# A Fourier-mixing and SoLU block on one core: shared even and odd up products, block transposes, and down products by Strassen's scheme

## The chip, the cores and the metric

The kernel runs on one core of a Trainium2 chip, in one launch, in float32 throughout. The metric is the device time of one execution in microseconds (us), median of several. Before the change it is 2172.12 us (three runs, 2170.49 to 2173.72). A profile is one further execution recorded by the hardware; its span is 2166.9 us.

A core has five engines with an instruction queue each: TensorE (PE, matrix products into PSUM), VectorE (DVE), ScalarE (ACT), GpSimd (POOL) and SyncE (SP, which here only issues transfers). They meet through semaphores. PSUM has eight banks of 512 float32 per partition.

## The reference, cut to what matters

```python
x: (8, 3136, 256)                                  # batch, sequence, features
X = np.fft.fft(np.fft.fft(x, axis=1), axis=2).real # 25088 tokens of 256 features
h = X @ w_in                                       # 256 -> 1024
e = np.exp(h - h.max(-1)); sm = e / (e.sum(-1) + 1e-9)
solu = h * sm
ln = (solu - mean(solu)) / np.sqrt(var(solu) + 1e-6) * g_ln
out = ln @ w_out                                   # 1024 -> 256
```

## The kernel before

The sequence transform (length 3136 = 49 x 64) is done in two passes of matrix products, for four pairs of batches. The feature transform is folded into `w_in`. A pair has 25 values of k1; each gives 64 frequencies for both batches, that is 128 tokens, and for k1 > 0 also the 128 tokens of the negative frequencies. In this text a *unit* is one (pair, k1) and a *block* is 128 tokens of one sign: 100 units, 196 blocks, 96 units of two blocks.

The first pass (`fold`, `transform1`) of the next pair runs in small steps beside the units of the current one, and goes through DRAM (`zd`) to turn its layout. The second pass gives `q`, the unit's 256 folded features on partitions:

```python
    def transform2(pr, k1):
        ps = ps_m.tile([P, KD, P], FP32, tag="m", name="ps2")
        for h in range(KD):
            nc.tensor.matmul(ps[:, h, :], pr.g[:, k1, ...], T[:, k1, :], ...)     # 2 products of 128 columns
        q = {"+": qpool.tile(...)}
        nc.vector.tensor_copy(out=q["+"], in_=ps)
        if k1:                                   # the sine half changes its sign for the negative frequencies
            ...
                nc.scalar.activation(out=o, in_=i, func=ACT.Copy, scale=sg if h else 1.0)
        return q
```

The second part handles one block at a time; `cur` is the block that enters and `prv` the one before it:

```python
    def up_half(t, half):                        # both halves: 4 products of 512 columns per block
        for h in range(KD):
            nc.tensor.matmul(t.h[:, fs], t.q[:, h, :], Wi[:, h, fs], start=(h == 0), stop=(h == KD - 1))

    def solu(t):
        nc.vector.tensor_reduce(out=nmax, in_=t.h, axis=AX.X, op=ALU.max, negate=True)
        nc.scalar.activation(out=t.u, in_=t.h, func=ACT.Exp, bias=nmax, accum_out=esum)
        nc.vector.scalar_tensor_tensor(out=t.u, in0=t.h, scalar=1.0, in1=t.u, ..., accum_out=usum)
        nc.gpsimd.tensor_scalar(out=nmean, in0=usum, scalar1=-1.0 / FF, ...)
        nc.scalar.activation(out=sq, in_=t.u, func=ACT.Square, bias=nmean, accum_out=ssq)
        ...                                      # four small operations on GpSimd give rs, 1 / deviation

    def transpose(t):                            # 8 transposes on TensorE, copied out by ScalarE and VectorE
        for half in range(2):
            tp = ps_t.tile([P, n, P], FP32, tag="t", name="tp")
            ...
    def down(t):
        ps = ps_m.tile([P, D], FP32, tag="m", name="ps_o")
        for c in range(KF):                      # 8 products of 256 columns per block
            nc.tensor.matmul(ps, t.uT[:, c, :], Wo[:, c, :], start=(c == 0), stop=(c == KF - 1))
        nc.vector.tensor_scalar(out=ot, in0=ps, scalar1=t.rs, scalar2=None, op0=ALU.mult)
        ...                                      # two stores of 64 rows

            if cur: up_half(cur, 0)
            if prv: transpose(prv)
            if cur:
                up_half(cur, 1)
                solu(cur)
                if cur.s == "+":
                    ...                          # transform2 of the next unit
                    ahead(pairs[cur.p + 1], cur.k1)      # fold or one transform1 step of the next pair
            if prv: down(prv)
```

PSUM: two `h` tiles of two banks, two banks for `tp` (`ps_t`), and two banks `ps_m` that `ps1` (the result of `transform1`), `ps2` and `ps_o` take in turn. Before the loop, the weights, which come as the bits of float64 numbers, are narrowed to float32 on VectorE, after the first pair's first pass.

Of the kernel before, what the change touches and what calls it, by code (L numbers as in the profile page):

```python
# [10 lines left out]
I32 = mybir.dt.int32  # L11
ALU = mybir.AluOpType
# [4 lines left out]
P = 128  # L17
# The sequence index is n = N2 * n1 + n2 and its frequency k = k1 + N1 * k2.
# The frequencies k1 of 0..NK-1 are computed; k1 and N1 - k1 share their products.
# [5 lines left out]
CH = 8  # L25
NC = NH // CH

# The layout of the 256 folded features: cosine part at 0..128, sine part (1..127) at 129..255.
# [4 lines left out]
def kernel(  # L33
# [13 lines left out]
    """Sequence DFT with even and odd folds, feature DFT folded into w_in, then SoLU and its layer norm.  # L47

    With U the cosine transform over the sequence of x folded evenly in the features, and V the sine
    transform of x folded oddly, the real part of the 2D DFT is U C - V S at frequency k and U C + V S  # L50
    at -k. So h = [U, V] @ [C w_in; -S w_in], and for -k the features of V change their sign.
    """
# [10 lines left out]
    out_b = out.rearrange("(b s) d -> b s d", b=B)  # L63
# [4 lines left out]
    gpool = ctx.enter_context(tc.tile_pool(name="gpool", bufs=2))  # L68
    qpool = ctx.enter_context(tc.tile_pool(name="qpool", bufs=3))
    small = ctx.enter_context(tc.tile_pool(name="small", bufs=4))  # L70
    dram = ctx.enter_context(tc.tile_pool(name="dram", bufs=2, space=bass.MemoryType.DRAM))
    ps_h = ctx.enter_context(tc.tile_pool(name="ps_h", bufs=2, space=PSUM))
    ps_t = ctx.enter_context(tc.tile_pool(name="ps_t", bufs=2, space=PSUM))
    ps_m = ctx.enter_context(tc.tile_pool(name="ps_m", bufs=2, space=PSUM))

    F = const.tile([PR, 6, ZR], FP32, name="F")
    T = const.tile([P, NK, P], FP32, name="T")
    Wi = const.tile([P, KD, FF], FP32, name="Wi")
    Wo = const.tile([P, KF, D], FP32, name="Wo")
    ident = const.tile([P, P], FP32, name="ident")  # L80
    ones = const.tile([P, P], FP32, name="ones")
    neg_half = const.tile([P, 1], FP32, name="neg_half")
    idx = const.tile([PR, NP * NC], I32, name="idx")
    sg = const.tile([P, 1], FP32, name="sg")

# [1 line left out]

    class Pair:
        def __init__(self, p):
            self.p = p  # L90
            self.raw, self.y, self.y0 = {}, {}, None
            self.g = None

    def load(pr, c):
        """Rows n2 = 8c + 1 .. 8c + 8, and those of S - n beside them (in descending order of n2)."""
        r = slice(pr.p * PR, (pr.p + 1) * PR)
        xa = xpool.tile([PR, CH, D], FP32, tag="xa", name="xa")
        xb = xpool.tile([PR, CH, D], FP32, tag="xb", name="xb")
        nc.sync.dma_start(out=xa, in_=x_pn[r, c * CH + 1 : (c + 1) * CH + 1, :])
        i = pr.p * NC + c  # L100
        nc.gpsimd.indirect_dma_start(
            out=xb.rearrange("p l d -> p (l d)"), out_offset=None, in_=x_g,
            in_offset=bass.IndirectOffsetOnAxis(ap=idx[:, i : i + 1], axis=0))
        x0 = None
        if c == NC - 1:
            x0 = xpool.tile([PR, 1, D], FP32, tag="x0", name="x0", bufs=1)
            nc.sync.dma_start(out=x0, in_=x_pn[r, 0:1, :])
        pr.raw[c] = (xa, xb, x0)

    def fold_features(o, i):  # L110
# [3 lines left out]
        nc.vector.tensor_copy(out=o[:, :, 0:129:128], in_=i[:, :, 0:129:128])  # L114

    def fold(pr, c):
        """x[n, d] + x[-n, -d], then its even and odd parts in d. Rows n2 = 0 and 32 hold their own mirrors."""
        xa, xb, x0 = pr.raw.pop(c)
        n = CH - 1 if c == NC - 1 else CH
        a, rb = xa[:, 0:n, :], xb[:, ::-1, :][:, 0:n, :]  # L120
        nc.gpsimd.tensor_tensor(out=a[:, :, 1:D], in0=a[:, :, 1:D], in1=rb[:, :, D - 1 : 0 : -1], op=ALU.add)  # L121
        nc.gpsimd.tensor_tensor(out=a[:, :, 0:1], in0=a[:, :, 0:1], in1=rb[:, :, 0:1], op=ALU.add)
        y = xpool.tile([PR, CH, D], FP32, tag="y", name="y")
        fold_features(y, xa)
        pr.y[c] = y
        if c == NC - 1:
            pr.y0 = xpool.tile([PR, 1, D], FP32, tag="y0", name="y0", bufs=1)
            fold_features(pr.y0, x0)

    def transform1(pr, s):  # L130
        """Sum over n1 for rows n2 = 2s + 1, 2s + 2; out: (b, cosine or sine, k1) on partitions.

        The last row holds n2 = 0, of no sine part, in its cosine part and n2 = 32 in its sine part."""
# [3 lines left out]
        if l == 0:  # L137
            pr.z = zpool.tile([ZR, CH, D], FP32, tag="z", name="z")
        y = pr.y[c]
        ps = ps_m.tile([P, 2, D], FP32, tag="m", name="ps1")  # L140
        if s == NH // 2 - 1:
            parts = [(ps[0:ZR, 0], y[:, l], 0), (ps[0:ZR, 1], pr.y0[:, 0], 1), (ps[0:ZR, 1], y[:, l + 1], 2)]
        else:
            parts = [(ps[0:ZR], y[:, l : l + 2], 0)]
        first = True
# [6 lines left out]
        if l == CH - 2:  # L152
            nc.sync.dma_start(out=pr.zd[:, c * CH : (c + 1) * CH, :], in_=pr.z)

    def turn(pr):
        """(b, cosine or sine, n2) onto partitions."""
        pr.g = gpool.tile([P, NK, D], FP32, tag="g", name="g")
        for j in range(4):
            nc.sync.dma_start(out=pr.g[j * NH : (j + 1) * NH, :, :],
                              in_=pr.zd[j * NK : (j + 1) * NK, :, :].rearrange("k n d -> n k d"))  # L160

    def transform2(pr, k1):
        """Sum over n2 for both batches; out: folded features on partitions, tokens (b, k2) free."""
        ps = ps_m.tile([P, KD, P], FP32, tag="m", name="ps2")
        for h in range(KD):
            nc.tensor.matmul(ps[:, h, :], pr.g[:, k1, h * P : (h + 1) * P], T[:, k1, :],  # L166
                             start=(h == 0), stop=(h == KD - 1), skip_group_check=True)
        q = {"+": qpool.tile([P, KD, P], FP32, tag="q", name="q")}
        nc.vector.tensor_copy(out=q["+"], in_=ps)  # L169
        if k1:  # L170
            # -(k1 + 49 k2) is (49 - k1) + 49 (63 - k2): the negative frequencies run backwards.
            q["-"] = qpool.tile([P, KD, P], FP32, tag="qm", name="qm")
            for h in range(KD):
                o = q["-"][:, h, :].rearrange("p (b k) -> p b k", b=2)
                i = ps[:, h, :].rearrange("p (b k) -> p b k", b=2)[:, :, ::-1]
                nc.scalar.activation(out=o, in_=i, func=ACT.Copy, scale=sg if h else 1.0)  # L176
        return q

# [1 line left out]

    class Tokens:
        def __init__(self, p, k1, s):
            self.p, self.k1, self.s = p, k1, s

    def up_half(t, half):
        if half == 0:
            t.h = ps_h.tile([P, FF], FP32, tag="h", name="h")
        fs = slice(half * HW, (half + 1) * HW)
        for h in range(KD):
            nc.tensor.matmul(t.h[:, fs], t.q[:, h, :], Wi[:, h, fs], start=(h == 0), stop=(h == KD - 1))  # L190

    def solu(t):
        """u = h exp(h - max h), its sum and centred sum of squares, and the sum of the exponentials."""
        nmax = small.tile([P, 1], FP32, tag="nmax", name="nmax")
        nc.vector.tensor_reduce(out=nmax, in_=t.h, axis=AX.X, op=ALU.max, negate=True)  # L195
        t.u = fpool.tile([P, FF], FP32, tag="u", name="u")
        esum = small.tile([P, 1], FP32, tag="esum", name="esum")
        nc.scalar.activation(out=t.u, in_=t.h, func=ACT.Exp, bias=nmax, accum_out=esum)  # L198
        usum = small.tile([P, 1], FP32, tag="usum", name="usum")
        nc.vector.scalar_tensor_tensor(out=t.u, in0=t.h, scalar=1.0, in1=t.u, op0=ALU.mult, op1=ALU.mult,  # L200
                                       accum_out=usum)
        nmean = small.tile([P, 1], FP32, tag="nmean", name="nmean")
        nc.gpsimd.tensor_scalar(out=nmean, in0=usum, scalar1=-1.0 / FF, scalar2=None, op0=ALU.mult)  # L203
        sq = fpool.tile([P, FF], FP32, tag="sq", name="sq", bufs=1)
        ssq = small.tile([P, 1], FP32, tag="ssq", name="ssq")
        nc.scalar.activation(out=sq, in_=t.u, func=ACT.Square, bias=nmean, accum_out=ssq)  # L206
        # 1 / (sum * sqrt(var(u / sum) + 1e-6)) = (var(u) + 1e-6 sum^2) ** -0.5
        es = small.tile([P, 1], FP32, tag="es", name="es")
        nc.gpsimd.tensor_scalar(out=es, in0=esum, scalar1=1e-9, scalar2=1e-3, op0=ALU.add, op1=ALU.mult)
        es2 = small.tile([P, 1], FP32, tag="es2", name="es2")  # L210
        nc.gpsimd.tensor_tensor(out=es2, in0=es, in1=es, op=ALU.mult)
        v = small.tile([P, 1], FP32, tag="v", name="v")
# [238 lines left out]
```

## Time and profile before

| | |
|---|---|
| time, median of 3 | 2172.12 us |
| span of the profile | 2166.9 us |
| TensorE busy | 1788.7 us |
| VectorE busy | 846.8 us |
| ScalarE busy | 670.6 us |
| GpSimd busy | 382.0 us |
| first `ps_o` product starts | 151.1 us |

How to read what follows. A line such as `L235 PE MATMUL ps_o<-Wo,uT 128*128 128x256 f32 x3136 | 833.5, 425 | 270.8 <- ...` is a group of instructions of line 235: engine, operation, output and inputs by their names in the program, shape, count; then the busy time in us and the mean of one in ns; then the idle time of the engine just before them and what ended it. A float32 product appears as two records: 1568 down products are 3136 records. Records of TensorE overlap (each ends long after the next began), so the time that a stretch takes is read from the distance of starts, not from the durations. PEld is the load of the stationary operand, which runs beside the products. In the row of 40 slices a digit is a busy share in tenths (9 is 90% or more), and PEclk is the clock that TensorE was granted, in tenths of full speed.

### The profile page before, as it was taken

How to read it: one execution, taken by the hardware profiler on the slowest of the kernel's cores; microseconds unless marked ns; L12 is line 12 of the kernel's file. 1: busy time of each engine (PE TensorE's matmuls, PEld its weight loads, DVE VectorE, ACT ScalarE, POOL GpSimd, SP SyncE). 2: the span in 40 equal slices, each digit the busy share in tenths (PEclk: the TensorE clock that was granted, in tenths of full speed). 3: DMA queues.
4: the chain of work that ended last, by engine and by line, in shares of the span. 5: the costliest groups of instructions: out<-in, count | busy, mean ns of one | idle time of the engine just before them, and what ended most of it. 6: DMA issues, size and time to landing. Idle time of an engine off the chain costs nothing. (4 is left out here: it accounts for less than half of the span.)

```text
span 2166.9 us, 19414 instructions
## 1 busy us (share of the span) xinstructions
PE 1788.7 (83%) x6992; PEld 1238.2 (57%) x6992; DVE 846.8 (39%) x1327; ACT 670.6 (31%) x1240; POOL 382.0 (18%) x1034
## 2 busy tenths in 40 slices
PE   2357888788799878878879987887887999999998
PEld 1135555555566555555556755555555666777666
DVE  2853233323334323332433433333233344444444
ACT  1113223223333322332332323233233234434443
POOL 3002121212112212121211221212121111111111
PEclk8679899889899888888999988889899899999999
DMA  9511010001042101000104210101010400000000
GB/s 240 133 33 42 24 46 13 25 13 28 10 90 75 42 20 50 12 26 12 28 11 88 77 42 16 54 10 28 11 29 11 88 18 18 17 16 18 18 18 17
DMA packets 56783, 84.78 MB, mean 39 GB/s; under 512 B 12038, under 2 KB 50574, under 8 KB 51696
## 3 DMA queue, kind: packets, MB, share of 16 engines
q1 hardware_dynamic: 48528, 65.19, 12.7%
q0 software_dynamic: 2048, 12.85, 2.1%
q10 hardware_dynamic: 6112, 5.52, 1.3%
q8 instruction: 55, 0.90, 0.2%
q14 instruction: 40, 0.33, 0.1%
HBM read 44.72 MB, written 38.80 MB: 39 GB/s over the span
## 5 line engine op out<-in xcount | busy, mean ns | idle before, releaser
L235 PE MATMUL ps_o<-Wo,uT 128*128 128x256 f32 x3136 | 833.5, 425 | 270.8 <-ACT qm L176 215.9
L235 PEld LDWEIGHTS ps_o<-Wo,uT 128*128 128x128 f32 x3136 | 668.7, 217 | 444.7 <-ACT qm L176 235.5
L198 ACT ACTIVATE u<-h,nmax 128x1024 f32<-128x1024 f32 x196 | 218.4, 1114 | 634.3 <-DVE nmax L195 634.3
L190 PE MATMUL h<-Wi,q 128*128 128x512 f32 x800 | 384.4, 604 | 7.8 <-DVE q L169 7.8
L190 PE MATMUL h<-Wi,qm 128*128 128x512 f32 x768 | 361.1, 592 | 0.0
L200 DVE SCALAR_TENSOR_TENSOR u<-h,u 128x1024 f32<-128x1024 f32 x196 | 240.0, 1225 | 249.4 <-ACT u L198 249.4
L206 ACT ACTIVATE sq<-u,nmean 128x1024 f32<-128x1024 f32 x196 | 225.1, 1148 | 317.7 <-POOL nmean L203 317.7
L195 DVE TENSOR_REDUCE nmax<-h 128x1 f32<-128x1024 f32 x196 | 239.9, 1224 | 193.5 <-PE h L190 193.5
L203 POOL TENSOR_SCALAR nmean<-usum 128x1 f32<-128x1 f32 x196 | 45.7, 233 | 1515.3 <-DVE u L200 1515.3
L228 DVE COPY uT<-tp 128x512 f32<-128x512 f32 x196 | 135.5, 691 | 372.3 <-PE tp L224 372.3
L230 ACT COPY uT<-tp 128x512 f32<-128x512 f32 x196 | 114.9, 586 | 415.9 <-PE tp L224 415.9
L224 PEld LDWEIGHTS tp<-ident,u 128*128 128x128 f32 x1568 | 183.5, 141 | 104.5 <-issue 103.7
L237 DVE TENSOR_SCALAR ot<-ps_o,rs 128x256 f32<-128x256 f32 x196 | 94.0, 480 | 369.4 <-issue 364.3
L190 PEld LDWEIGHTS h<-Wi,q 128*128 128x128 f32 x800 | 147.5, 195 | 115.4 <-issue 103.7
L224 PE MATMUL tp<-ident,u 128*128 128x128 f32 x1568 | 203.2, 273 | 0.5 <-DVE u L200 0.5
L190 PEld LDWEIGHTS h<-Wi,qm 128*128 128x128 f32 x768 | 138.4, 190 | 96.8 <-issue 91.8
L215 POOL TENSOR_TENSOR rs<-v,neg_half 128x1 f32<-128x1 f32 x196 | 113.2, 578 | 16.3
L148 PE MATMUL ps<-y,F 98*100 98x258 f32 (+3 forms) x288 | 71.5, 385 | 43.3 <-DVE y L114 43.3
L166 PEld LDWEIGHTS ps<-T,g 128*128 128x128 f32 x400 | 60.4, 191 | 47.4 <-issue 47.4
L213 POOL TENSOR_SCALAR v<-ssq,es 128x1 f32<-128x1 f32 x196 | 52.4, 267 | 177.6 <-ACT sq L206 175.5
L148 PEld LDWEIGHTS ps<-y,F 98*100 98x100 f32 x288 | 45.5, 178 | 54.7 <-DVE y L114 30.4
L121 POOL TENSOR_TENSOR xa<-xa,xb 98x2040 f32<-98x2040 f32 (+1 forms) x16 | 70.1, 4379 | 28.9 <-DMA xa<-in_x_dram 16.2
(50 smaller groups left out, 544.4 us busy)
## 6 DMA issues: line engine op xcount, KB each, us to landing
out_dram<-ot SPq DMA_DIRECT2D x392, 64.0 KB
zd<-z SPq DMA_DIRECT2D x16, 800.0 KB
g<-zd SPq DMA_DIRECT2D x16, 800.0 KB
xa<-in_x_dram SPq DMA_DIRECT2D x16, 784.0 KB
raw_in_moe_w_in_dram<-in_moe_w_in_dram ACTq DMA_DIRECT2D x1, 2048.0 KB
raw_in_moe_w_out_dram<-in_moe_w_out_dram ACTq DMA_DIRECT2D x1, 2048.0 KB
T<-in_t_tab_dram ACTq DMA_DIRECT2D x2, 400.0 KB
x<-in_x_dram SPq DMA_DIRECT2D x4, 98.0 KB
```

The source lines that it names most:

```text
L148: nc.tensor.matmul(o[..., cs], F[:, 2 * t + h, :], i[..., cs], start=first, stop=True, skip_group_check=True)
L190: nc.tensor.matmul(t.h[:, fs], t.q[:, h, :], Wi[:, h, fs], start=(h == 0), stop=(h == KD - 1))
L195: nc.vector.tensor_reduce(out=nmax, in_=t.h, axis=AX.X, op=ALU.max, negate=True)
L198: nc.scalar.activation(out=t.u, in_=t.h, func=ACT.Exp, bias=nmax, accum_out=esum)
L200: nc.vector.scalar_tensor_tensor(out=t.u, in0=t.h, scalar=1.0, in1=t.u, op0=ALU.mult, op1=ALU.mult, accum_out=usum)
L206: nc.scalar.activation(out=sq, in_=t.u, func=ACT.Square, bias=nmean, accum_out=ssq)
L215: nc.gpsimd.tensor_tensor(out=t.rs, in0=v, in1=neg_half, op=ALU.pow)
L224: nc.tensor.matmul(tp[:, c, :], t.u[:, f * P : (f + 1) * P], ident, is_transpose=True, start=(c == 0), stop=(c == n - 1), skip_group_check ...
L228: nc.vector.tensor_copy(out=o, in_=tp)
L230: nc.scalar.copy(o, tp)
L235: nc.tensor.matmul(ps, t.uT[:, c, :], Wo[:, c, :], start=(c == 0), stop=(c == KF - 1))
L237: nc.vector.tensor_scalar(out=ot, in0=ps, scalar1=t.rs, scalar2=None, op0=ALU.mult)
```

## The change

The products of both signs are shared. With E the part of h from the cosine features and O the part from the sine features, h is E + O for one sign and E - O for the other, so each part is computed once per unit. One feature (the middle one) moves from the cosine half to a separate per-token term `w_mid * r`. VectorE then builds both h in SBUF and takes their maxima as it does so. The transposes leave TensorE: VectorE transposes blocks of 32 x 32 within SBUF, and 16 transfers per two units carry the blocks to their partitions. The down products of both signs of a unit form one product of a 256 x 1024 matrix (two signs) with a 1024 x 256 matrix; it is cut into 2 x 2 blocks and done by seven block products in place of eight. Sums of blocks of u are formed on GpSimd, sums of weights once, and results on three PSUM banks; the seven products are spread over two steps of the loop, four units behind the one that enters. The diff is cut to its core; in the loop, conditions are left out and calls condensed.

```diff
@@ parameters, pools @@
-CH = 8
+CH = 4
-    ps_h = ctx.enter_context(tc.tile_pool(name="ps_h", bufs=2, space=PSUM))
-    ps_t = ctx.enter_context(tc.tile_pool(name="ps_t", bufs=2, space=PSUM))
-    ps_m = ctx.enter_context(tc.tile_pool(name="ps_m", bufs=2, space=PSUM))
+    ps_h = ctx.enter_context(tc.tile_pool(name="ps_h", bufs=1, space=PSUM))
+    ps_m = ctx.enter_context(tc.tile_pool(name="ps_m", bufs=1, space=PSUM))
... (first pass: smaller pieces; turn in five parts per pair, on GpSimd's queue)
@@ a unit of both signs @@
+    def up(t, c):
+        ps = ps_h.tile([P, FF], FP32, tag=f"h{c}", name=f"ps_h{c}")
+        for half in range(2):
+            nc.tensor.matmul(ps[:, fs], t.q[:, c * P : (c + 1) * P], Wi[:, c, fs], start=True, stop=True)
+    def even(t, ps):
+        nc.vector.scalar_tensor_tensor(out=t.ev, in0=w_mid, scalar=t.r, in1=ps, op0=ALU.mult, op1=ALU.add)
+    def join(t, s):
+        nc.vector.tensor_tensor_reduce(out=t.h[s], in0=t.h[0] if s else t.ev, in1=t.odd, scale=1.0 if s else -0.5,
+                                       scalar=-3.0e38, op0=ALU.add, op1=ALU.max, accum_out=t.nmax[:, s : s + 1])
+    def expo(t, s):
+        nc.scalar.mul(out=t.neg[:, s : s + 1], in_=t.nmax[:, s : s + 1], mul=-1.0)
+        nc.scalar.activation(out=t.u[s], in_=t.h[s], func=ACT.Exp, bias=t.neg[:, s : s + 1], accum_out=...)
+    def product(t, s):
+        nc.vector.scalar_tensor_tensor(out=t.u[s], in0=t.h[s], scalar=1.0, in1=t.u[s], ..., accum_out=...)
+    def square(t, s):
+        nc.scalar.activation(out=t.h[s], in_=t.u[s], func=ACT.Square, bias=t.usum[...], scale=-float(FF), accum_out=...)
+    def stats(t):
+        ... (one Square and, per sign, one Identity on ScalarE; one power on GpSimd)
+    def turn_blocks(t, s):
+        for o in (s,) if len(t.signs) == 2 else (0, 1):
+            nc.vector.transpose(out=t.batch.v[:, t.w, :, o], in_=t.u[s])
+    def move_blocks(batch, units, engines=(nc.sync,)):
+        for i in range(4):
+            for q in range(4):
+                engines[i % len(engines)].dma_start(out=uT[b, i], in_=v[a, q])
@@ down products of both signs @@
+    def sums(t):
+        for o, a, b, op in ((t.S[:, 0], A21, A22, ALU.add), (t.S[:, 1], t.S[:, 0], A11, ALU.subtract),
+                            (A21, A11, A21, ALU.subtract), (t.S[:, 2], A12, t.S[:, 1], ALU.subtract)):
+            nc.gpsimd.tensor_tensor(out=o, in0=a, in1=b, op=op)
+    def product7(o, a, b, start=False):
+        for c in range(KF // 2):
+            nc.tensor.matmul(o, a[:, c], b[:, c], ...)
+        def p1(self):
+            product7(self.C11, self.A11, Wo[:, 0 : KF // 2, 0:P], True)
+            nc.scalar.copy(self.C21, self.C11)
+        def p5(self):
+            product7(self.P53, self.t.S[:, 0], Ws[:, 0], True)
+            nc.scalar.copy(self.E5, self.P53)
+        def p6(self):
+            product7(self.C21, self.t.S[:, 1], Ws[:, 1])
+            nc.scalar.copy(self.X, self.C21)
+        def p2(self):
+            product7(self.C11, self.A12, Wo[:, KF // 2 :, 0:P])
+            self.scale(0, 0, self.C11)
+        def p7_p3(self):
+            product7(self.C21, self.S3, Ws[:, 2])
+            product7(self.P53, self.t.S[:, 2], Wo[:, KF // 2 :, P:])
+        def sum22(self): nc.vector.tensor_tensor(out=self.C22, in0=self.C21, in1=self.E5, op=ALU.add)
+        def sum12(self): nc.vector.tensor_tensor(out=self.C12, in0=self.P53, in1=self.X, op=ALU.add)
+        def p4(self):
+            product7(self.C21, self.A22, Ws[:, 3])
+            ... (three scalings on ScalarE)
+    def store(t):
+        ... (one indirect store on GpSimd's queue and one on SyncE's per unit)
@@ the loop, from unit 5 on (`old` is four units behind `cur`, `half` one more) @@
+            square(prv), stats(prv)
+            sums(nxt)
+            ps = up(cur, 0)
+            half.p4(); half = Down(old, ...); half.p1()
+            other_pairs(i, ahead_pe)             # a transform1 step of the next pair
+            even(cur, ps)
+            half.p5()
+            store(units[i - lag - 1])
+            cur.odd = up(cur, 1); join(cur, 0)
+            half.p6(); expo(cur, 0); half.p2()
+            second_transform(i + 2)
+            join(cur, 1); expo(cur, 1)
+            half.p7_p3(); product(cur, 0); half.sum22(); product(cur, 1); half.sum12()
+            turn_blocks(cur, s) for both signs; after every second unit move_blocks(...)
+            other_pairs(i, ahead)                # loads and folds of the next pair
```

Units 0 to 3 still take TensorE transposes; the units with k1 = 0 and the very last unit still take plain down products. The preparation is rearranged too: the narrowing of the weights (fewer operations each, partly on ScalarE) now stands between the first pair's folds instead of after them, the result of the first pair's first pass is stored and turned in parts, and the tables of the second transform load in two parts.

## The prediction

> **What bounds the kernel now.** I read the page's shares and its row of slices first, then the chain that ended last, a stretch of TensorE's timeline, the groups by form, and the waits.
>
> ```profile
> PE 1788.7 (83%) x6992; PEld 1238.2 (57%) x6992; DVE 846.8 (39%) x1327; ACT 670.6 (31%) x1240; POOL 382.0 (18%) x1034
> ...
> PE   2357888788799878878879987887887999999998
> ...
> PEclk8679899889899888888999988889899899999999
> ```
>
> TensorE is the only engine near full. It is full with a clock of 0.9 to 1.0 in the last quarter (the last pair, with no first pass beside it), and at 8 tenths with a clock of 8 to 9 tenths before.
>
> ```profile
> 1794.27 3.46 PE ps_o L235 x16
> 1802.03 3.45 PE ps_o L235 x16
> 1810.24 3.46 PE ps_o L235 x16
> ```
>
> The chain in the last pair holds nothing but TensorE. Two blocks, one unit, take 1810.24 - 1794.27 = 15.97 us. The timeline says of what:
>
> ```profile
> 1805.32 1.88 PE L190 MATMUL h<-Wi,q 128*128 128x512 f32 x4
> 1807.04 1.04 PE L224 MATMUL tp<-ident,u 128*128 128x128 f32 x8
> 1807.91 1.88 PE L190 MATMUL h<-Wi,q 128*128 128x512 f32 x4
> 1809.63 0.61 PE L166 MATMUL ps<-T,g 128*128 128x128 f32 x4
> 1810.07 3.62 PE L235 MATMUL ps_o<-Wo,uT 128*128 128x256 f32 x16
> 1813.53 1.88 PE L190 MATMUL h<-Wi,qm 128*128 128x512 f32 x4
> ```
>
> From starts: half an up product 1.72 us, eight transposes 0.87, transform2 0.44, a down product 3.46. So a record of 512 columns repeats every 0.43 us, one of 256 every 0.216, one of 128 every 0.11: time goes by columns. A unit is 4 x 1.72 + 2 x 0.87 + 0.44 + 2 x 3.46 = 15.98, as the chain says.
>
> ```profile
> PE ps_o L235 <- ACT qm L176: 215.9, 48, 4.5
> ```
>
> (Total us, times, longest us.) The other loss before the last pair is a PSUM bank: in the 48 steps with `ps1`, the down product takes the bank of `ps2` and waits for its copies, 4.5 us each; with 54 us behind `uT` that makes 270. The whole adds up: 96 x 15.98 + 4 x 8.2 = 1567, first pass in the loop 48 x 0.86 = 41, waits 270, about 141 before the loop (first `ps_o` at 151.1); of 2167 us some 148 remain, which I give to the lower clock.
>
> **What the Trainium skill says.** "TensorE: Matmul & The Clock Gate", LDWEIGHTS: loading 128 columns takes 128 / 1.2 GHz = 107 ns. Here every record has a load, and 128-column records repeat every 0.109 to 0.11 us: agreement, and no room, as load and stream are just equal there. The same page, Part 1: idle gaps of some 3.4 us drop the clock. The stretch 1850 to 1900 us shows a granted clock of 1.00 with TensorE never idle, 1280 to 1330 shows 0.84 with the 4.5 us waits: agreement. "SBUF — State Buffer", Who interferes with whom: a VectorE operation with two SBUF inputs and a GpSimd operation that reads SBUF exclude each other. The loop before never pairs them (its large VectorE operations read PSUM), so no number here shows it. "DMA: Bandwidth & Descriptors", Why small descriptors are slow: the penalty is said to hold for HBM only. The table T arrives here as 3200 packets of 256 B, median 32 ns and mean 43 ns a packet, beside other loads; nothing here moves from SBUF to SBUF.
>
> **The change, part by part.** For a unit of two blocks:
>
> *TensorE.* Up products: 4 instead of 8 of 512 columns, 3.44 us instead of 6.88: -3.44. Transposes leave: -1.74. Down: 28 products of 128 columns, 56 records x 0.11 = 6.2, instead of 6.92: only -0.75, since 7/8 is all that the scheme can give. transform2 stays at 0.44. Sum 3.44 + 6.2 + 0.44 = 10.0, and 10.9 in the 48 units that carry a transform1 step (4 records of 256 columns, 0.86).
>
> *VectorE.* The durations come from the groups by form:
>
> ```profile
> L200 DVE SCALAR_TENSOR_TENSOR u<-h,u 128x1024 f32<-128x1024 f32 x196 | 240.0, 1225 | 249.4 <-ACT u L198 249.4
> L195 DVE TENSOR_REDUCE nmax<-h 128x1 f32<-128x1024 f32 x196 | 239.9, 1224 | 193.5 <-PE h L190 193.5
> L206 ACT ACTIVATE sq<-u,nmean 128x1024 f32<-128x1024 f32 x196 | 225.1, 1148 | 317.7 <-POOL nmean L203 317.7
> L198 ACT ACTIVATE u<-h,nmax 128x1024 f32<-128x1024 f32 x196 | 218.4, 1114 | 634.3 <-DVE nmax L195 634.3
> L121 POOL TENSOR_TENSOR xa<-xa,xb 98x2040 f32<-98x2040 f32 x12 | 54.2, 4514 | 25.7 <-DMA xa<-in_x_dram 13.0 <-DMA xb<-in_x_dram,idx 12.7
> L176 ACT ACTIVATE qm<-ps,sg 128x128 f32<-128x128 f32 x96 | 34.3, 357 | 0.0
> L176 ACT ACTIVATE qm<-ps 128x128 f32<-128x128 f32 x96 | 24.6, 256 | 0.0
> L121 POOL TENSOR_TENSOR xa<-xa,xb 98x1785 f32<-98x1785 f32 x4 | 15.9, 3972 | 3.3 <-DMA xa<-in_x_dram 3.3
> ```
>
> Seven passes of 1024 columns per unit (even, two joins, two products, two block transposes; I estimate the join and the transpose at the rate of the others, no row shows them) at 1.15 us from start to start (an L200 starts at 1221.17, its accumulator read at 1222.32) are 8.05, and two sums of 128 columns 0.28 each (L112 took 283 ns for 127): 8.6. Before it was 2 x (1.23 + 1.22 + 0.69 + 0.48 + 0.08) + 0.42 = 7.8 per unit. Two waits join it: the first product waits for the exponential of the sign joined before, which with its negation takes about 0.5 us longer than the second join; the second waits behind a scaling, the copy of q, a negation and an exponential, 2.2 us against 1.4 of VectorE work. Chain: 8.6 + 0.5 + 0.8 = 9.9. Folds add 1.4 in 24 of the steps.
>
> *ScalarE.* Exponentials 2 x (1.11 + 0.19), squares 2 x (1.15 + 0.19) = 5.3; three copies at 0.26, four scalings at 0.36, q at 0.37, five tiny operations at 0.15 to 0.25: 3.6. Sum 8.9; with the copy of transform1 (0.59) 9.5.
>
> *GpSimd.* Its slope is (4514 - 3972) / 255 = 2.13 ns per column, its fixed part 0.18 us: four sums of 512 columns 4 x 1.27 = 5.1. Power 0.6, indirect store 1.4, first pass of the next pair (mirror sums, gathers, turning) about 2.2 on average. Sum 9.3, from under 4 before.
>
> So TensorE leads with 10.0 to 10.9, VectorE's chain has 9.9 to 11.3, and two more engines 9: the work is spread evenly, and the bound is a loop through four engines. I **choose** 10.4 us for the 24 units of the last pair, 11.3 with transform1, 10.6 else: (24 x 10.4 + 48 x 11.3 + 20 x 10.6) / 92 = 10.9. The 270 us of waits go, as banks no longer change roles (h0, h1, transforms on m0, down on the others), and with gaps under 1 us I expect a clock of 0.95 or more.
>
> *Before the loop.* Weights were narrowed after the first pass, VectorE 47 of 50 us busy from 60 to 110. Now both are interleaved. Loads of some 9 MB at about 240 GB/s take 37 us, VectorE's work to the first unit about 47; first up product near 65 us. The first five units go through TensorE transposes, nearly in series: one sign 8, then four at 12: 56.
>
> *After it.* The last four units have only down products, 7 us each and a little for the last: 32.
>
> Sum: 65 + 56 + 92 x 10.9 + three units of one sign in the loop at 8 + 32 = 1180 of span; the median lies 5 us over the profile's span (2172.1 against 2166.9): **1185 us**.
>
> **Rivals.** *(a) GpSimd and VectorE exclude each other.* For: 5.1 us of GpSimd sums per unit read SBUF, and the two products have both inputs there (`even` and the joins have one in PSUM). Against: sums are issued at the start of a step and products stand at its end, over 5 us later. If each product waits for one sum: 2 x 1.2 us x 92 = +220, about 1400; likelier is a quarter of that. *(b) The block transfers bound.* Two units move 8192 packets of 256 B, 512 per engine of sixteen. At the median of 32 ns that is 16 us per two units of 21.8; at the mean of 43 it is 22 and, with loads and stores, some 26: 13 us per unit, near 1370. For: nothing as fine-grained moved before. Against: the slow packets of T shared the engines with large loads; the fastest tenth took 18 ns. Four units of lag hide latency, not rate. *(c) Weight loads bound the small products.* With 0.13 us in place of 0.11 a record the 56 records cost 1.1 more, +100: 1285. Against: transposes and transform2 already run at 0.11. *(d) The ring of small waits.* Within a step copies on ScalarE release products p6 and p2, whose results go back to ScalarE before the exponential. If each of some six handovers shows 0.2 us, a unit takes 12: 1290.
>
> **Range and chances.** TensorE's columns alone allow nothing below about 1080: 92 x 10.0, 41 for transform1, 65 before the first product and some 50 for the other units. Rivals c and d in half measure make 1240, b or a in full 1370 to 1400. I take 1110 to 1290. Even rival a leaves it a third faster, so slower than now would need an error that no row hints at.
>
> **What would show it.** In the profile after: about 7000 records on TensorE (68 a unit) and a busy share near 0.9; PEclk at 9 throughout; a unit every 10.4 us late in the chain; 0.11 us per record in the seven products; VectorE's passes still at 1.2 us (longer means rival a); a DMA row of 5 to 8 tenths (9 means b); waits of TensorE for ScalarE's copies under 0.5 us each (more means d). Wrong it would be above all through the step length: a tenth of a us per unit is 9 us.

## The result, and the profile after

The changed kernel takes **1312.99 us** (median of four runs, 1307.94 to 1320.03) against 2171.3 us for the kernel before on the same chip: ratio **0.6047, 95% interval 0.6025 to 0.607**. Predicted were 1185 us, 1110 to 1290. The direction holds, the time lies above the range, 128 us over the sum.

The page of the changed kernel first: busy times, the rows of 40 slices, and the shares of the span in the chain of work that ended last (SPq is SyncE issuing transfers):

```profile
PE 1175.4 (90%) x7002; PEld 918.2 (70%) x7002; DVE 1045.8 (80%) x1425; ACT 840.2 (64%) x2175; POOL 930.7 (71%) x750
...
PE   2988988979998898999998889989999989999997
...
PEclk9999999989998999999999989998999999999999
DMA  9655767747577676645669667874475657555553
...
PE 28%; DVE 19%; DMA 16%; SPq 14%; issue 10%; ACT 9%; POOL 4%; DVEq 0%; ACTq 0%; POOLq 0%
```

About 7000 records on TensorE and a share near 0.9 were predicted, and a DMA row of 5 to 8 tenths, which has a few 4s. But TensorE still drops to 7 and 8 tenths in the first three pairs, and there the clock row has some 8s. And the chain is not TensorE's alone: the 14% of SPq are the issues of the blocks of u, and 8% more are their landings. What a unit's step takes is read from the starts of `even`, one per unit (us of the span):

| Stretch | predicted | after |
|---|---|---|
| first `even` (predicted: first up product) | 65 | 59.9 |
| first five units | 56 | 42.8 |
| loop, from the sixth `even` to the last | 1016 | 1159 |
| rest | 42 | 45.3 |
| mean step, units 25 to 75 (pairs two and three) | 10.9 | 12.8 |
| mean step, last pair | 10.3 | 10.75 |

(The prediction's 92 x 10.9 and three units at 8 include the last unit's own 10.4 us; here that stands in the rest.) The loop is 143 us over, and 18 are won back before it. Most of the 143 lies where the first pass of the next pair runs beside the units; the last pair has 11. The groups by form (idle time before them last) name a first suspect:

```profile
L268 DVE SCALAR_TENSOR_TENSOR u<-h,u 128x1024 f32<-128x1024 f32 x196 | 330.2, 1686 | 41.5 <-ACT u L261 40.6
L300 DVE STREAM_TRANSPOSE v<-u 128x1024 f32<-128x1024 f32 x192 | 226.7, 1217 | 0.0
L350 POOL TENSOR_TENSOR S<-uT 128x512 f32<-128x512 f32 x95 | 150.6, 1586 | 173.6 <-DMA r<-q 71.9 <-DMA out_dram<-ot 59.8 <-DMA xa<-in_x_dram 18.1
L350 POOL TENSOR_TENSOR S<-S,uT 128x512 f32<-128x512 f32 x95 | 149.7, 1575 | 7.5
L252 DVE CUSTOM_DVE_ANT_0 h<-ev,ps_h 128x1024 f32<-128x1024 f32 x100 | 122.2, 1222 | 153.8 <-PE ps_h L238 147.8
```

The same product `h * u` that took 1225 ns in the kernel before takes 1686. The sums on GpSimd take 1.45 to 1.59 us against the estimate of 1.27. VectorE's other passes have their 1.22 us. In the last pair one sees the two meet, start and duration first:

```profile
1104.65 1.50 POOL L350 TENSOR_TENSOR S<-uT 128x512 f32<-128x512 f32 x1
1104.90 2.33 DVE L268 SCALAR_TENSOR_TENSOR u<-h,u 128x1024 f32<-128x1024 f32 x1 [0.17 <-ACT u L261]
1106.23 2.17 POOL L350 TENSOR_TENSOR S<-S,uT 128x512 f32<-128x512 f32 x1
...
1107.37 2.10 DVE L268 SCALAR_TENSOR_TENSOR u<-h,u 128x1024 f32<-128x1024 f32 x1
...
1108.36 2.02 POOL L350 TENSOR_TENSOR uT<-uT 128x512 f32<-128x512 f32 x1
```

The durations can be taken apart: an operation that starts while another runs waits for its end and then needs nearly its own time. The first sum ends at 1106.15, the product begun at 1104.90 ends 1.08 us later, at 1107.23; the second sum ends 1.17 after that, the second product 1.07 after that sum (1109.47), the third sum 0.91 after the product (1110.38). They take turns, whole operation by whole operation, and each duration after the first is a wait and a run. The waits (total us, times, longest us) name a second suspect:

```profile
DVE h L252 <- PE ps_h L238: 147.8, 65, 7.9
...
PE ps_m L182 <- ACT ps_m L383: 44.4, 19, 3.0
...
PE ps_m L182 <- DVE y L129: 11.8, 10, 2.0
...
PE ps_m L182 <- DVE y L128: 9.9, 3, 5.0
```

L182 is `transform1`, L128 and L129 are the fold that it reads, and L252 is the join, which waits for an up product. One such step from the timeline:

```profile
489.73 2.35 DVE L300 STREAM_TRANSPOSE v<-u 128x1024 f32<-128x1024 f32 x2
492.02 0.64 DVE L128 TENSOR_TENSOR y<-xa 98x508 f32<-98x508 f32 x1
492.58 0.67 DVE L129 TENSOR_TENSOR y<-xa 98x508 f32<-98x508 f32 x1
492.80 1.18 PE L182 MATMUL ps_m<-y,F 98*100 98x258 f32 x4 [3.03 <-ACT ps_m L383]
495.42 2.84 PE L238 MATMUL ps_h<-Wi,q 128*128 128x512 f32 x4
498.39 1.22 DVE L252 CUSTOM_DVE_ANT_0 h<-ev,ps_h 128x1024 f32<-128x1024 f32 x1 [3.95 <-PE ps_h L238]
```

The fold stands at the end of VectorE's step, after the transposes. TensorE reaches `transform1` early in the next step, stands for 3.03 us, then does `transform1`, p5 and half an up product, the last in 2.84 us where 1.88 is its usual record, and the join waits 3.95. The wait names a copy of ScalarE (L383) that ended at 492.70, next to the first half of the fold at 492.66; which of them was waited for the row can't tell.

### The profile page after: what moved, and what is told of

It reads as the page before. It is cut to its first block, busy times and chain, and to the rows that moved or that the text cites. A ratio compares the mean times of both kernels' runs of the same rounds, so it can differ in the third digit from the quotient of the medians. Undisturbed runs are those within 1.5% of the kernel's fastest.

```text
span 1307.4 us, 21623 instructions
## 1 busy us (share of the span) xinstructions
PE 1175.4 (90%) x7002; PEld 918.2 (70%) x7002; DVE 1045.8 (80%) x1425; ACT 840.2 (64%) x2175; POOL 930.7 (71%) x750
## 3 DMA queue, kind: packets, MB, share of 16 engines
q0 software_dynamic: 13760, 38.16, 11.3%
## 4 chain that ended last, share of the span: by engine, by line
PE 28%; DVE 19%; DMA 16%; SPq 14%; issue 10%; ACT 9%; POOL 4%; DVEq 0%; ACTq 0%; POOLq 0%
SPq L326 14%; PE ps_m L355 13%; PE ps_h L238 9%; DMA uT<-v 8%; DVE u L268 6%; DVE v L300 5%; DMA out_dram<-ot 3%; DVE h L252 3%; ACT h L275 2%; ACT u L261 2%; PE ps_m L182 2%; POOL S L350 2%; DMA room<-in_x_dram 2%; PE ps_m L421 1%; DVE y L129 1%
## 5 line engine op out<-in xcount | busy, mean ns | idle before, releaser
L238 PE MATMUL ps_h<-Wi,q 128*128 128x512 f32 x800 | 393.3, 616 | 0.8 <-DVE nmax L252 0.8
L268 DVE SCALAR_TENSOR_TENSOR u<-h,u 128x1024 f32<-128x1024 f32 x196 | 330.2, 1686 | 41.5 <-ACT u L261 40.6
L275 ACT ACTIVATE h<-u,usum 128x1024 f32<-128x1024 f32 x196 | 224.6, 1146 | 75.3 <-DVE u L268 73.9
L355 PEld LDWEIGHTS ps_m<-Ws,S 128*128 128x128 f32 x1520 | 206.5, 203 | 74.5 <-issue 46.7
L252 DVE CUSTOM_DVE_ANT_0 h<-ev,ps_h 128x1024 f32<-128x1024 f32 x100 | 122.2, 1222 | 153.8 <-PE ps_h L238 147.8
L355 PEld LDWEIGHTS ps_m<-Ws,uT 128*128 128x128 f32 x1520 | 200.4, 196 | 48.8 <-issue 28.9
L355 PE MATMUL ps_m<-Ws,S 128*128 128x128 f32 x1520 | 219.1, 291 | 12.6 <-POOL S L350 7.2
L261 ACT ACTIVATE u<-h,neg 128x1024 f32<-128x1024 f32 x196 | 225.5, 1151 | 6.4
L300 DVE STREAM_TRANSPOSE v<-u 128x1024 f32<-128x1024 f32 x192 | 226.7, 1217 | 0.0
L355 PE MATMUL ps_m<-Wo,uT 128*128 128x128 f32 x1520 | 212.4, 283 | 15.0 <-issue 3.6
L355 PE MATMUL ps_m<-Ws,uT 128*128 128x128 f32 x1520 | 210.9, 282 | 2.3 <-DVE E L402 2.3
L355 PEld LDWEIGHTS ps_m<-Wo,uT 128*128 128x128 f32 x1520 | 195.5, 197 | 18.4 <-ACT ot L414 4.2
L182 PE MATMUL ps_m<-y,F 98*100 98x258 f32 (+3 forms) x288 | 82.7, 419 | 90.9 <-ACT ps_m L383 44.4
```

The source lines that it names most:

```text
L182: nc.tensor.matmul(o[..., cs], F[:, 2 * t + h, :], i[..., cs], start=first, stop=True, skip_group_check=True)
L238: nc.tensor.matmul(ps[:, fs], t.q[:, c * P : (c + 1) * P], Wi[:, c, fs], start=True, stop=True)
L252: nc.vector.tensor_tensor_reduce(out=t.h[s], in0=t.h[0] if s else t.ev, in1=t.odd, scale=1.0 if s else -0.5, scalar=-3.0e38, op0=ALU.add, ...
L261: nc.scalar.activation(out=t.u[s], in_=t.h[s], func=ACT.Exp, bias=t.neg[:, s : s + 1], accum_out=t.esum[:, s : s + 1])
L268: nc.vector.scalar_tensor_tensor(out=t.u[s], in0=t.h[s], scalar=1.0, in1=t.u[s], op0=ALU.mult, op1=ALU.mult, accum_out=t.usum[:, s : s + 1])
L275: nc.scalar.activation(out=t.h[s], in_=t.u[s], func=ACT.Square, bias=t.usum[:, s : s + 1], scale=-float(FF), accum_out=t.ssq[:, s : s + 1])
```

## The experiments

Two theories. **F**: `transform1` stands in TensorE's order before p5 and the second up product, and waits for a fold that VectorE has only just done; the gap also costs clock. **P**: products and sums exclude each other, as rival (a) had it, in nearly all units. All kernels below are edits of the changed kernel; times are medians, ratios are to the kernel before.

**1. `transform1` one step later.**

```diff
 def ahead_pe(pr, step):
-                if step == START[pr.p == 1][c] + 2 + half:
+                if step == START[pr.p == 1][c] + 3 + half:
```

> Both transform1 steps of a piece stand one step later, so that TensorE never meets a fold that VectorE has just begun; nothing else changes. Theory F (TensorE stands behind the fold of the step before, 24 times some 2 to 3 us, and then at a low clock): 50 to 90 us less, 1225 to 1265 us, and the waits of transform1 for the fold (about 90 us before it in all) gone. Theory P (VectorE and GpSimd shut each other out, and that alone sets the step): within 10 us of 1313.

1252.35 us, ratio 0.5778 (0.576 to 0.5795): 61 us less. The rows of L182 for the copy, L128 and L129 have left the waits, and the join's wait is more than halved:

```profile
DVE h L252 <- PE ps_h L238: 67.5, 42, 5.7
...
PE ps_m L182 <- DVE y L130: 24.7, 5, 18.3
```

(The row that remains is from before the loop.) The copy L383 was not moved relative to `transform1`, only the fold was, so the fold was the wait. Steps of units 25 to 75 fall from 12.8 to 11.6 us, the clock rises from 0.964 to 0.983, and the last pair, which has no `transform1`, stays (10.75 and 10.93). F holds.

**2. No sums.** `S` is replaced by the weight tile `Ws`, so the kernel leaves out the four GpSimd sums per unit and multiplies other data; all else stays.

```diff
-        t.S = spool.tile([P, 3, KF // 2, P], FP32, tag="S", name="S")
-        for o, a, b, op in (...): nc.gpsimd.tensor_tensor(out=o, in0=a, in1=b, op=op)
+        t.S = Ws
```

> The four sums of u per unit on GpSimd are left out (the products take weight sums in their place, so the output is another). Theory P: the product u falls from a mean of 1.69 us to 1.23, some 90 us of VectorE time go, and with them 60 to 100 us of the whole: 1215 to 1255. Theory F: the waits of transform1 stay, the time falls by less than 30 us: above 1285.

1220.44 us, ratio 0.5618 (0.5608 to 0.5628): 93 us less, and the product is nearly back at its duration of before (1225 ns):

```profile
L268 DVE SCALAR_TENSOR_TENSOR u<-h,u 128x1024 f32<-128x1024 f32 x196 | 244.0, 1246 | 62.5 <-ACT u L261 58.8 <-issue 3.6
```

**3. Sums that only write.** Experiment 2 takes away GpSimd's work as well as the meeting. Here four memsets of 1536 columns, of about the sums' length, stand in their place; the sums themselves are left out.

```diff
-        for o, a, b, op in (...): nc.gpsimd.tensor_tensor(out=o, in0=a, in1=b, op=op)
+        for _ in range(4):
+            nc.gpsimd.memset(t.S, 0.0)
```

> In place of the four sums GpSimd writes a constant over the three sum blocks four times, 1536 columns each, which keeps it about as busy but reads nothing (the sums are left out, the output is another). If GpSimd's reads shut VectorE out (theory P), the product u is at 1.23 us and the time is that of the run without sums within 15 us. If it is GpSimd's occupation, whatever it does (its later instructions come late), the time stays within 20 us of 1313.

1249.74 us, ratio 0.5758 (0.5749 to 0.5768): between the two expectations, so the total missed both. The groups by form of 960 to 1180 us, in the last pair, are clear all the same:

```profile
L349 POOL MEMSET S<- 128x1536 f32 x80 | 110.2, 1378 | 3.5
L268 DVE SCALAR_TENSOR_TENSOR u<-h,u 128x1024 f32<-128x1024 f32 x43 | 52.7, 1226 | 13.9 <-ACT u L261 8.0 <-issue 5.9
```

GpSimd is busy for 155 of these 220 us (with the sums it was 142 of 180), and 20 of the 43 products run beside a memset, yet the product takes 1226 ns and a step 10.36 us. It is GpSimd's reading that lengthens the product, not its work. From 400 to 900 us the product had 1543 ns. There the first pass's mirror sums, which read, also run on GpSimd:

```profile
475.25 2.38 POOL L137 TENSOR_TENSOR xa<-xa,xb 98x1020 f32<-98x1020 f32 x1
475.45 3.27 DVE L268 SCALAR_TENSOR_TENSOR u<-h,u 128x1024 f32<-128x1024 f32 x1 [0.17 <-ACT u L261]
```

Of the 83 products in that stretch 14 took more than 1.3 us, up to 4.1, and every one of these overlaps a mirror sum. In experiment 2, without memsets in GpSimd's queue, it was one of 83. That is the part that the expectation had left out. What this run does not separate is why sums cost time: a memset, unlike a sum, also need not wait for the blocks of u.

**4. Plain down products.** To see what the seven products bring, `seven` is set false and the sums are left out, at the places the code has for it.

```diff
-            if nxt and len(nxt.signs) == 2:       # the sums
+            if False:
-            seven = old and len(old.signs) == 2 and old is not units[-1]
+            seven = False
```

> The down products of every unit are plain ones of 256 columns, no sums and no block products; all else as in the changed kernel. TensorE has 0.75 us more per unit, VectorE two small sums and ScalarE three copies less, GpSimd loses its 5 us of sums. Theory P: what the seven products save on TensorE they lose on VectorE; the time is 1230 to 1310, not above the changed kernel. If TensorE's columns set the step (my prediction's view): 1313 + 70 = 1360 to 1390.

1544.21 us, ratio 0.7113 (0.7101 to 0.7125), far outside. The comparison was not a fair one: both products stand in one place, and their scalings stand behind the next exponential, so the next step's products wait for banks, and `transform1` waits for folds as never before:

```profile
PE ps_m L182 <- DVE y L128: 170.4, 24, 7.3
```

This is from the waits; the groups give the down products themselves another 53.9 us of idling for the scalings. What it shows is the price of placing: TensorE's records are those of experiment 7 (4720), with edit 1 and better places there, and this is 326 us slower.

**5. Both causes away**, edits 1 and 2 together; the sums are left out.

```diff
-                if step == START[pr.p == 1][c] + 2 + half:
+                if step == START[pr.p == 1][c] + 3 + half:
-        for o, a, b, op in (...): nc.gpsimd.tensor_tensor(out=o, in0=a, in1=b, op=op)
+        t.S = Ws
```

> Both at once: transform1 one step later, and the four sums left out (weight sums stand in, so the output is another). If the wait behind the fold (60 us in the first run) and the exclusion (92 us in the second) are two separate causes that account for the miss, their effects add, apart from steps in which one hid the other: 1160 to 1190 us, my predicted 1185 within it. If they are one cause seen twice: above 1210.

1180.29 us, ratio 0.5451 (0.5431 to 0.5471). The loop takes 1031 us where 1016 were predicted, the rest 40.9 where 42 were. From here each cause can be sized in both orders: the sums cost 93 us with the early `transform1` (1313.0 - 1220.4) and 72 with the late one (1252.4 - 1180.3); the early `transform1` costs 61 with the sums and 40 without (1220.4 - 1180.3). They overlap by 20 us; together they are 133. The 72 to 93 us are for the sums in all: for meeting the products and for coming late.

**6. Sums held back.** If the meeting is the cost, sums that begin right after the products should be free. They are moved to the head of GpSimd's step, behind a tiny operation that reads the last product's sum (on top of edit 1).

```diff
+            if nxt and len(nxt.signs) == 2:
+                held = small.tile([P, 1], FP32, tag="held", name="held", bufs=1)
+                nc.gpsimd.tensor_scalar(out=held, in0=prv.usum[:, n - 1 : n], scalar1=1.0, scalar2=None, op0=ALU.mult)
+                sums(nxt)
             square(prv), stats(prv)
-            sums(nxt)
```

> transform1 one step later, and the four sums of a step start when the second product of the step before has ended (a tiny GpSimd operation reads its sum first), ahead of the power and the store, so that they run beside the block transposes, even and the joins, which have one SBUF input at most. The arithmetic is unchanged. Theory P: the mean of the product u falls from 1.74 to 1.3 to 1.45 us and the time from 1252 to 1190 to 1225; what is left is steps in which the transfers of uT come late and the sums with them. If only the amount of GpSimd work counts and not its place: 1245 to 1260.

1258.46 us, ratio 0.5799 (0.5789 to 0.5809): no gain, a miss. The timeline shows why:

```profile
1052.70 0.28 POOL L785 TENSOR_SCALAR held<-usum 128x1 f32<-128x1 f32 x1
1052.90 1.55 POOL L350 TENSOR_TENSOR S<-uT 128x512 f32<-128x512 f32 x1
1052.93 2.61 DVE L268 SCALAR_TENSOR_TENSOR u<-h,u 128x1024 f32<-128x1024 f32 x1 [0.17 <-ACT u L261]
1054.53 2.16 POOL L350 TENSOR_TENSOR S<-S,uT 128x512 f32<-128x512 f32 x1
...
1055.67 2.10 DVE L268 SCALAR_TENSOR_TENSOR u<-h,u 128x1024 f32<-128x1024 f32 x1
```

The hold had been satisfied long before; GpSimd arrives late. The sums' first operation idles for 131.9 us, of which 91 are put down to landings of transfers (`r<-q`, `out_dram<-ot`) that share SyncE's queue with the blocks. SyncE needs about 0.85 us for each of the 16 issues, over 13 us for two units and more than a step, and then the last block still has to land.

**7. Plain down products, well placed.** Edit 1, no sums, one sign at the place of p5 and the other at that of p6, three banks in rotation, each scaling behind the exponential that follows it. Nothing is left out of the result.

```diff
-                ps_o = [down(old, s) for s in order]
+                ps_o = [down(old, order[0])]          # at p5's place
             cur.odd = up(cur, 1); join(cur, 0)
+                ps_o.append(down(old, order[1]))      # at p6's place
             expo(cur, 0)
+                scale(old, order[0], ps_o[0])
             second_transform(i + 2); join(cur, 1); expo(cur, 1)
+                scale(old, order[1], ps_o[1])
```

> Plain down products once more, but placed fairly: transform1 one step later; the first sign's product where p5 stood, the second after the odd half of up, results going round three banks, each scaled behind an exponential, so that no bank is waited for. The 1544 us of the first plain version came from both products waiting for one scaling each step, if I read its profile rightly; then this one takes 1210 to 1260: TensorE 10.8 to 11.7 us per unit, VectorE under 10. So the seven products would have brought nothing over it in their present placement (1252), and some 60 us at best once the exclusion is gone. If plain products are slow by their columns: above 1290.

**1218.4 us**, ratio 0.5618 (0.5608 to 0.5627): the fastest version that computes all. From the chain that ended last, in the last pair (start, us, work):

```profile
1010.93 1.72 PE ps_h L238 x4
1012.65 3.45 PE ps_m L422 x16
1016.11 1.72 PE ps_h L238 x4
1017.82 3.45 PE ps_m L422 x16
1021.27 0.44 PE ps_m L210 x4
1021.72 1.72 PE ps_h L238 x4
```

A unit in 1021.72 - 1010.93 = 10.79 us and nothing but TensorE, busy 96% of the span. So the seven products with their sums were not only short of their gain: against the same base (experiment 1) they cost 34 us. Without the sums (experiment 5) they are 38 us faster than this.

**8. One transfer for sixteen.** The blocks of two units move in one transfer of the same 2 MB, so they arrive unturned and the down products see other data (on top of edit 1).

```diff
-        for i in range(4):
-            for q in range(4):
-                engines[i % len(engines)].dma_start(out=uT[b, i], in_=v[a, q])
+        engines[0].dma_start(out=uT, in_=v)
```

> transform1 one step later, and the sixteen transfers of 256 B pieces per two units replaced by one transfer of the same 2 MB in pieces of 16 KB; the blocks then stay on their partitions, so the output is another. Issue on SyncE falls from some 13 us per two units to about 1. If late transfers push the sums into the products and hold up TensorE: 1205 to 1235, and the waits of the sums for transfers gone. If the transfers are hidden by the lag of four units: within 10 us of 1252.

1250.85 us, ratio 0.5755 (0.5735 to 0.5775): the whole is as in experiment 1, so rival (b), by which the rate of the transfers bounds the kernel, falls. But the step is not unchanged inside: units 25 to 75 rise from 11.6 to 12.0 us, the last pair falls from 10.93 to 10.35. Beside the first pass sums now begin earlier and meet the fold instead (400 to 500 us; min, median, max ns):

```profile
L129 DVE TENSOR_TENSOR y<-xa x4: 1982/1987/1997, 401.4 to 478.5; 98x508 f32<-98x508 f32 x4
```

Alone it takes 679 ns (experiment 7). Products still met sums: 1731 ns on average, and in the last pair (1004 to 1184 us) no less:

```profile
L268 DVE SCALAR_TENSOR_TENSOR u<-h,u 128x1024 f32<-128x1024 f32 x34 | 59.3, 1743 | 4.0 <-ACT u L261 4.0
```

There 17 of the 34 products meet a sum and take 2.28 us, and still nearly every step from the eighth on takes 10.3 us, as in experiment 5, which has no sums. With the blocks there in time, then, the longer product costs the last pair's step nothing. Where they come late (experiment 1) the steps scatter from 9.7 to 15.2.

**9. Held sums and one transfer**, edits 6 and 8 on edit 1; blocks again unturned.

```diff
+                nc.gpsimd.tensor_scalar(out=held, in0=prv.usum[:, n - 1 : n], ...)
+                sums(nxt)
...
+        engines[0].dma_start(out=uT, in_=v)
```

> Both edits together: the sums are held back until the products of the previous step are done (as in e6), and the blocks of u of two units move in one transfer of the same bytes (as in e8, blocks not turned), on top of the later transform1. Theory P with late transfers: in e6 the hold was useless because the transfers, 16 issues of 0.85 us, brought the blocks half a step late, so that the sums began late and fell on the products again. With the blocks there in time the held sums should lie in the first half of a step, the product u should return to 1.25 to 1.35 us and the run to 1180 to 1215. Rival: GpSimd is late for other reasons (mirror sums, indirect stores, the power), the hold alone cannot place the sums; then the product stays near 1.7 us and the run within 15 us of e6 and e8, 1240 to 1270.

1221.97 us, ratio 0.5633 (0.5616 to 0.5651): 7 us over the range of P, 18 under that of the rival. In the last pair, the groups of 965 to 1145 us:

```profile
L268 DVE SCALAR_TENSOR_TENSOR u<-h,u 128x1024 f32<-128x1024 f32 x34 | 41.7, 1226 | 10.9 <-ACT u L261 10.7 <-POOL S L347 0.2
L347 POOL TENSOR_TENSOR S<-uT,S 128x512 f32<-128x512 f32 x18 | 23.5, 1303 | 0.0
```

With the data there and the hold in force, real sums leave the product at 1226 ns, and a step takes 10.28 us. That the sums can be had for nothing is thus shown for the last pair; by experiment 8 the early data alone do that there, the hold adds under 0.1 us. Over the whole kernel it takes both: from experiment 1 the hold alone changed +6 us, the one transfer alone -2, both -30. Beside the first pass the sums are not free: a step takes 11.6 us against 11.0 without them (experiment 5, units 25 to 75), and from 350 to 900 us the product had 1588 and the fold's second half 1641 ns, where mirror sums, gathers and turns also stand in GpSimd's queue.

**10. Mixed.** Edits 1 and 6, but seven products only for the second unit of each batch of two, whose blocks have two steps to arrive; the first takes the plain products of experiment 7. Nothing is left out.

```diff
-            if nxt and len(nxt.signs) == 2:
+            if nxt and len(nxt.signs) == 2 and i % 2 == 0:
-            seven = old and len(old.signs) == 2 and old is not units[-1]
+            seven = old and len(old.signs) == 2 and old is not units[-1] and i % 2 == 1
```

> Seven products and held sums only for the second unit of each batch of two, whose blocks have two steps from transfer to sums; the first unit of a batch takes plain down products, placed as in e7, on the banks of C11 and P53. transform1 later as in e1. Theory P with late transfers: half as many sums, all with their data in time, so the product u stays at 1.25 to 1.35 us; TensorE does 10.0 us in one unit and 10.7 in the next instead of 10.7 in each, so 46 x 0.5 to 0.7 us less than e7 (1218.4): 1185 to 1205. Rival: the sums cost on GpSimd and the copies on ScalarE what TensorE gains, the product goes to 1.5 us or more in half of the units, and the run lies within 10 us of e7 or above it, 1215 to 1245.

1224.95 us, ratio 0.5642 (0.5633 to 0.5652): no gain over experiment 7, as the rival had it, but not for the rival's reason. In the last pair the products are back at 1225 ns, but steps alternate between 9.7 and 11.8 us. Two starts of `even` bound the short one:

```profile
1050.94 1.24 DVE L244 SCALAR_TENSOR_TENSOR ev<-w_mid,r,ps_h 128x1024 f32<-128x1024 f32 x1
...
1060.65 1.24 DVE L244 SCALAR_TENSOR_TENSOR ev<-w_mid,r,ps_h 128x1024 f32<-128x1024 f32 x1
```

Between them VectorE never pauses for more than 0.5 us: its own chain needs 9.7 us. TensorE has about 9.2 in the step that takes six of the seven products (3.44 + 0.44 + 48 x 0.11) and more in the other, which takes the seventh besides its own two. What it saves in the first is lost in waiting for VectorE.

## Why the prediction was wrong, by its own steps

**Held.** The method of the sum: with both causes away the whole is 1180 us against 1185. That it is so near is luck in part: the loop takes 1031 us against 1016, and the time before it 102 against 121. TensorE's share is right; in experiment 5's last pair a steady step is 10.3 us (chosen 10.4). Groups of eight records in the seven products start 0.89 to 0.95 us apart there, 0.11 to 0.12 a record; rival (c) falls. Joins and block transposes take 1.22 us each, as estimated. VectorE's chain, worked out as 9.9, is 9.7 (experiment 10). Waits for PSUM banks as in the kernel before are gone.

**Failed: rival (a), "sums are issued at the start of a step and products stand at its end, over 5 us later".** Issued is not started. GpSimd's sums wait behind the transfers of the blocks, the power and the mirror sums, and drift onto the products: in the changed kernel 25 of 33 in the last pair (1057 to 1237 us) overlap a sum. "Likelier is a quarter of" 220 would have been 55, and none of it was in the 1185; the runs show 72 to 93 for the sums in all. "Four units of lag hide latency" failed with it: the issues of two units take longer than a step, and blocks that come in time bring the last pair's step from 10.93 to 10.35 us with the products as long as before (experiments 1 and 8); the hold then adds under 0.1 us (experiment 9). Beside the first pass the meetings cost as well: with the blocks in time, the hold takes 0.45 us off a step of units 25 to 75 (12.04 to 11.59). The Trainium skill, page "SBUF — State Buffer", Who interferes with whom, has a two-input VectorE operation contend with a GpSimd operation that reads SBUF and not with one that only writes. The runs agree with both halves: 1686 ns on average in the changed kernel and up to 2.6 us beside the sums, 1226 beside memsets. It calls the contention an exclusive lock, and the turns in the timeline above show that: each operation waits for the end of the other.

**Failed: the step of "11.3 with transform1".** The fold was counted as 1.4 us of VectorE work and `transform1` as 0.86 us of TensorE columns. That TensorE, in program order, needs that fold early in the next step, while VectorE puts it last, was not looked at; the waits for `y` were not in any rival. It costs 40 to 61 us, part of it as clock: 0.93 from 400 to 600 us, against 0.99 in the last pair and 0.99 for the same stretch in experiment 1. The prediction had, from the Trainium skill, page "TensorE: Matmul & The Clock Gate", Part 1, that idle gaps of some 3.4 us drop the clock. Here shorter ones were followed by a drop too: after the 3.03 us above the granted clock was 0.50 from 494 to 497 us, and after a wait of 1.77 us for a fold (to 464.5) it was 0.50 from 467 to 470. The measurement decides.

**The rivals' other parts.** (b) falls as a bound by rate, yet the transfers matter by their time of arrival: their issues, about 0.85 us each, decide when sums begin. (d) was not tested by itself; at 10.3 us a step experiment 5 leaves no room for it.

What stays open is how the cost of sums beside the first pass splits between late data and meetings, and among products, folds and mirror sums; and whether the sixteen issues can be made fewer with the blocks still turned.

## What to carry to other kernels

When work goes to GpSimd beside a VectorE operation with two SBUF inputs, find out when it will start, from the last of its inputs and of its engine's earlier work, and not from its place in the program; then either give its data a step more or let it only meet operations with one SBUF input. Ask also which of the two costs time: in experiment 8's last pair products of 2.28 us in place of 1.23 cost the step nothing, while late blocks had cost it 0.6 us. For every product on TensorE that reads what another engine makes, compare the place of the maker in its own order with that of the reader: moving one product a step later gave 61 us. And set a saving of an eighth on one engine against the next engine's chain before paying for it: here plain products, placed well, beat the seven with their sums by 34 us.

## What the runs showed of the hardware

- A GpSimd sum of 512 columns takes 1.04 us in place and 1.30 otherwise when nothing is in its way, the first after a wait 1.52 (experiment 9, last pair), and 2.0 to 2.2 when it meets a VectorE product (the timeline of the changed kernel above); that product goes from 1.23 to as much as 2.6 us beside sums and to 4.1 beside a mirror sum (experiment 3), and the fold's half from 0.68 to 1.99 (experiment 8).
- A transfer of 128 KB within SBUF, in 512 packets of 256 B, keeps SyncE's queue for 0.81 us (experiment 7, last pair); one of 64 KB, at the end of experiment 7, for 0.65. Halving it cheapens the issue by a fifth only, while one of 2 MB in pieces of 16 KB takes 0.50 (experiment 8).
- After 3.03 us of idling TensorE was granted half its clock from 494 to 497 us and took 2.84 us for half an up product, 1.88 otherwise; a wait of 1.77 us was followed by half the clock as well.
